# Second expert layer of a fused attention and two-layer MLP kernel: slices over two chunks, six accumulators, single units

## The chip, the cores and the metric

One core of one Trainium2 chip runs the whole program in one launch. The metric is device time in microseconds. The engines have a queue each and run it in order: TensorE (PE in the rows, its weight loads PEld), VectorE (DVE), ScalarE (ACT), GpSimd (POOL) and SyncE (SP), whose queue here issues DMAs.

## What is computed

```python
attn = attention(q, k, v)              # q is averaged over pairs of rows first
x = attn as (1152 tokens, 512)
h = x @ w_in;  g = P(h) / Q(h);        x = g @ w_out      # first expert layer, d_ff 2048
h = x @ w2_in; g = max(h,0) + log1p(exp(-|h|)); out = g @ w2_out   # second expert layer
```

The weights come as 64-bit floats and are made into 32-bit pairs on the chip (below: decoding). Every product is made from a high and a low part of both factors, in three matmuls: high by high, low by high, high by low.

## The kernel before

After attention (to about 340 us) both expert layers run over three chunks `c` of 384 tokens (`NCH`, `TOK`) and 16 slices `f` of 128 hidden columns (`NF`), of which the first eight (`FH`) make the first half. A *unit* is one (c, f). For a unit, `up` (L600) makes h with 12 matmuls of 384 columns (4 blocks of the model dimension by three products); the activation follows on ScalarE and VectorE; `down1` (L648, 12 matmuls of 384 columns) or `down2` (L692, 9 of 512 columns) adds the unit to accumulators in PSUM. Units are taken in pairs of neighbouring slices of one chunk: h is a tile of two PSUM banks (L602) with two buffers, and an activation works on 768 columns at once.

In the first layer an activation is long. ScalarE runs `act1_a` (L625 to L628), VectorE `act1_y` (L633, L635, L634; the last frees h), ScalarE Ln and Exp (L639, L640), VectorE the products L644, L645, L646, then ScalarE makes the high part gh (L620) and VectorE the low part gl (L621, shown as L122, the line of the helper `sub`). Downs follow their ups by two pairs. At a chunk's end `end1` (L672) adds up the halves (L678), and ScalarE and VectorE split the sum into xh and xl for the next layer. In the second layer the activation is one softplus (L689), gh (L620) and gl (L122), and downs follow by one pair.

The second layer's first half today takes its units chunk by chunk: chunk 2 with slices 0 to 7, then chunk 1, then chunk 0 (L832). The accumulators of one chunk are three banks of four; at the end of a chunk's first half `half2` (L704) copies them to SBUF.

Decoding a weight tile is: a load of 512 KB into one of two raw buffers (L162 for w_in, L167 for w_out); a scaled copy on ScalarE (L174 in and after the last pair of the first layer, L176 before); L182, L185 (only after L174) and L188 on VectorE; then the split: a cast on ScalarE (L198) and a subtraction (L199, shown as L122). `w_step` (L758) does one piece of each for successive tiles: split one, convert the next, copy the one after, load the one after that. Three things call it: `w_pace` in the first layer, by the rates r0 (first half) and r1 (second half), in steps per hundred units; the rate r2 in the second layer; and `w_need`, which repeats it until a tile that is used next has been split. The subtraction of a split runs on VectorE in the first layer and on GpSimd from the last pair of the first layer on (L760).

The order of instructions on each engine is set by a scheduler, which moves them against the order in which the code issues them; `tc.high_priority` and `behind` (L112: issue after a named instruction) steer it. Each engine then runs its list in that order.

Of the kernel before, what the change touches and what calls it, by code (L numbers as in the profile page):

```python
# [7 lines left out]
F32 = mybir.dt.float32  # L8
# [61 lines left out]
    pra=0,  # L70
    k1=1,
    r0=50,
    r1=60,
    r2=60,
    whd=0,
    dup=2,
    qsp=0,
# [9 lines left out]
def attn_moe_kernel(tc, q, k, v, w1_in, w1_out, moe_a, moe_b, w2_in, w2_out, out):  # L87
# [24 lines left out]
    def behind(fn, *engines):  # L112
        with ExitStack() as es:
            for e in engines:
                es.enter_context(tc.issue_after(st["last", e]))
            fn()

    def sb(**kw):
        return tc.alloc_tile_pool(reuse_waits="tile", **kw)

    def sub(eng, o, a, b):
        return eng.tensor_tensor(out=o, in0=a, in1=b, op=ALU.subtract)  # L122
# [69 lines left out]
    def w_split(i, pool, lo):  # L192
        g = st.pop(("pk", i)).bitcast(F32)
        w = pool.tile([128, 2, 512], F32R, tag="w", name="w")
        if T["whd"] and i % T["whd"] == 0:
            nc.vector.tensor_copy(out=w[:, 0], in_=g)
        else:
            nc.scalar.copy(out=w[:, 0], in_=g)  # L198
        sub(lo, w[:, 1], g, w[:, 0])  # L199
        st["w", order[i]] = w  # L200
        st["wp", order[i]] = pool
# [392 lines left out]
    def xcols(c):  # L594
        return slice(c * TOK, (c + 1) * TOK)

    def T_(nm, bufs, dt=F32):
        return ap.tile([128, 2, TOK], dt, tag=nm, name=nm, bufs=bufs)

    def up(m, c, f):  # L600
        if f % 2 == 0:
            st["h"] = ph_.tile([128, 2, 512], F32, tag="h", name="h")[:, :, 0:TOK]  # L602
        h = st["h"][:, f % 2]
        w = st["w", (m, 0, f)]
        n = 0
        for d in range(ND):
            wd = slice(d * 128, (d + 1) * 128)
            for wi, x in ((0, xh), (1, xh), (0, xl)):
                nc.tensor.matmul(out=h, lhsT=w[:, wi, wd], rhs=x[:, d, xcols(c)],  # L609
                                 start=(n == 0), stop=(n == 3 * ND - 1))  # L610
                n += 1
        return st["h"]
# [1 line left out]
    def pick(key, n):  # L614
        return T[key][n % len(T[key])]

    def split(p, es=(slice(0, 2),)):
        gh, gl = T_("gh", 2, F32R), T_("gl", 2, F32R)
        for e in es:
            nc.scalar.copy(out=gh[:, e], in_=p[:, e])  # L620
            sub(nc.vector, gl[:, e], p[:, e], gh[:, e])  # L621
        return gh, gl

    def act1_a(h):
# [58 lines left out]
                    nc.scalar.copy(out=xh[:, d, xcols(c)], in_=t)  # L683
                sub(nc.vector, xl[:, d, xcols(c)], t, xh[:, d, xcols(c)])

    def act2(h, es=(slice(0, 2),)):
        p = T_("p", 2)
        for e in es:
            nc.scalar.activation(out=p[:, e], in_=h[:, e], func=AF.Softplus)  # L689
        return split(p, es)  # L690

    def down2(c, f, gh, gl, ts=(0, 1, 2)):  # L692
        first = f == 0 or (f == FH and c > 0)
        last = f == NF - 1 or (f == FH - 1 and c > 0)
        if first:
            for t in range(TOK // 128):
                st["acc", c, t] = pa_.tile([128, DM], F32, tag="acc", name="acc")
        w = st["w", (1, 1, f)]
        for t in ts:
            for n, (g, wi) in enumerate(((gh, 0), (gh, 1), (gl, 0))):  # L700
                nc.tensor.matmul(out=st["acc", c, t], lhsT=g[:, t * 128:(t + 1) * 128], rhs=w[:, wi],  # L701
                                 start=(first and n == 0), stop=(last and n == 2))

    def half2(c):  # L704
        p = st["part2", c] = pt2[c - 1].tile([128, TOK // 128, DM], F32, name=f"part2{c}")
        for t in range(TOK // 128):
            acc = st.pop(("acc", c, t))
            with tc.high_priority():
                if t == 1:
                    nc.vector.tensor_copy(out=p[:, t], in_=acc)  # L710
                else:
                    nc.scalar.copy(out=p[:, t], in_=acc)
# [16 lines left out]
    if True:  # L729
# [27 lines left out]

        def w_step():  # L758
            if cnt["split"] < cnt["conv"] and freed:
                w_split(cnt["split"], freed.pop(0), nc.gpsimd if "second" in st else nc.vector)  # L760
                cnt["split"] += 1
            if cnt["conv"] < cnt["abs"]:
                for n in range(3):
                    w_conv(cnt["conv"], n)
                cnt["conv"] += 1
            if cnt["abs"] < cnt["load"] and cnt["abs"] - cnt["split"] < 2:
                w_abs(cnt["abs"])
                cnt["abs"] += 1
            if cnt["load"] < len(order) and cnt["load"] - cnt["conv"] < 2:
                w_load(cnt["load"])  # L770
                cnt["load"] += 1

        def w_need(t):
            while cnt["split"] <= order.index(t):
                w_step()
# [11 lines left out]
        def every(n, rate):  # L787
            return (n + 1) * rate // 100 > n * rate // 100
# [40 lines left out]
                g1.pop(k - LAG1)  # L829
        pt_.release()  # L830
        pt2 = [sb(name=f"part2{c}", bufs=1) for c in range(2)]
        units = [(c, f) for c in reversed(range(NCH)) for f in range(FH)]  # L832
        units += [(c, f) for c in range(NCH) for f in range(FH, NF)]
        g2 = {}
        for k in range(NG + LAG2):
            if k < NG:
                for e, (c, f) in enumerate(units[2 * k:2 * k + 2]):
                    if c == (NCH - 1 if f < FH else 0):
                        w_need((1, 0, f))
                    h = up(1, c, f)  # L840
                    if f < FH and c == 0:
                        freed.append(st["wp", (1, 0, f)])
                    if e == 0 and every(2 * k, T["r2"]):
                        w_step()
                g2[k] = act2(h, (slice(0, 2),) if k < NG - 1 else (slice(0, 1), slice(1, 2)))
                if every(2 * k + 1, T["r2"]):
                    w_step()
            if k >= LAG2:
                for e, (c, f) in enumerate(units[2 * (k - LAG2):2 * (k - LAG2) + 2]):
                    if c == (NCH - 1 if f < FH else 0):  # L850
                        w_need((1, 1, f))
                    if c < NCH - 1 or f < NF - LAST:
                        gh, gl = g2[k - LAG2]
                        down2(c, f, gh[:, e], gl[:, e])
                        if f < FH and c == 0:
                            freed.append(st["wp", (1, 1, f)])
                        if f == FH - 1 and c:
                            half2(c)
                        if f == NF - 1:
                            for t in range(TOK // 128):  # L860
                                end2(c, t)
        for t in range(TOK // 128):
            for n in range(NU - LAST, NU):
                gh, gl = g2[n // 2]
                down2(*units[n], gh[:, n % 2], gl[:, n % 2], ts=(t,))
            end2(NCH - 1, t)
        pt2[1].release()
        pt2[0].release()
# [39 lines left out]
```

## Time and profile before

| | us |
|---|---|
| runs, median of three | 758.01 (754.85 to 762.01) |
| profiled execution | 755.56 |
| its span, first to last instruction | 753.8 |
| TensorE busy in the span | 726.2 (96%) |
| VectorE, ScalarE, GpSimd busy | 545.4, 494.4, 262.2 |

The span is 753.8 us of the profiled execution's 755.56; 1.8 us lie around it. Busy time is the union of an engine's instructions. Attention ends at about 340 us, the first expert layer at 551 us, and the second fills the rest. In a timeline, rows of the same kind that follow each other are merged (x2, x8), a bracket gives the engine's idle time just before the row and what ended it, and "q" rows are an engine's sequencer.

### The profile page before, as it was taken

Reading aid. Unit: us, or ns where it says so; the run is one execution under the profiler, and the core shown is the slowest. Engines: PE = TensorE matmul, PEld = TensorE weight load, DVE = VectorE, ACT = ScalarE, POOL = GpSimd, SP = SyncE. Lnnn points to the kernel's source line nnn. Section 1 sums busy time; section 2 is a strip of 40 time slices with the busy share of each in tenths; the row PEclk is TensorE's granted clock in tenths of the full one; section 3 lists DMA queues with packets and bytes.
Section 4 is the critical chain, followed back from the end, with each engine's and each line's share of the span. In section 5 each row is a group of like instructions: output and inputs, shape, how many; then the busy total and the mean of one; then the engine's idle time right before and its main releaser. Section 6 shows DMA issues by size and latency. Waiting matters only on the chain.

```text
span 753.8 us, 11735 instructions
## 1 busy us (share of the span) xinstructions
PE 726.2 (96%) x4273; PEld 682.4 (91%) x4273; DVE 545.4 (72%) x906; ACT 494.4 (66%) x921; POOL 262.2 (35%) x212
## 2 busy tenths in 40 slices
PE   8999999999999998887999999999999899999998
PEld 5699999999999998777999999999889779989996
DVE  6877778787867679988999999999987772111122
ACT  3278888888888889988767777876744452222121
POOL 5278796969697875000000000000233431000000
PEclk9999999999999999998999999999999999999999
DMA  4876383737353434331202122221224440001011
GB/s 131 205 154 153 94 188 84 185 85 185 84 126 85 98 99 127 125 128 57 84 29 80 61 84 62 81 82 56 85 93 138 138 137 0 1 1 43 0 43 43
DMA packets 60474, 70.32 MB, mean 93 GB/s; under 512 B 20008, under 2 KB 48512, under 8 KB 60416
## 3 DMA queue, kind: packets, MB, share of 16 engines
q1 hardware_dynamic: 59232, 68.58, 34.0%
q10 hardware_dynamic: 1184, 0.98, 0.4%
q8 instruction: 34, 0.56, 0.3%
q14 instruction: 24, 0.20, 0.1%
HBM read 47.71 MB, written 2.36 MB: 66 GB/s over the span
## 4 chain that ended last, share of the span: by engine, by line
PE 78%; DVE 11%; ACT 6%; issue 2%; DMA 2%; POOL 0%; DVEq 0%; ACTq 0%; SPq 0%
PE h L609 20%; PE p L396 11%; PE acc L659 11%; PE acc L701 10%; PE s L446 5%; PE s L447 5%; PE pv L471 5%; PE pv L469 4%; PE pv L470 4%; DVE pk L188 2%; DMA wraw<-in_moe_w_in_dram 2%; ACT p L450 1%; ACT ph L457 1%; DVE pk L182 1%; DVE pk L185 1%
## 5 line engine op out<-in xcount | busy, mean ns | idle before, releaser
L609 PE MATMUL h<-xh,w 128*128 128x384 f32 x768 | 198.9, 338 | 7.4 <-DVE p L634 7.4
L122 POOL TENSOR_TENSOR pl<-p,ph 128x576 fp32r<-128x576 f32 x126 | 181.4, 1453 | 55.0 <-ACT ph L457 35.5
L609 PEld LDWEIGHTS h<-xh,w 128*128 128x128 f32 x768 | 140.6, 190 | 10.2 <-issue 8.3
L401 DVE TENSOR_REDUCE nm<-p 128x1 f32<-128x384 f32 x216 | 117.0, 552 | 44.9 <-PE p L396 43.4
L450 ACT ACTIVATE p<-s 128x288 f32<-128x288 f32 x288 | 114.9, 408 | 28.4 <-PE s L447 26.6
L609 PE MATMUL h<-xl,w 128*128 128x384 f32 x384 | 129.8, 338 | 0.0
L122 POOL TENSOR_TENSOR w<-pk,w 128x512 fp32r<-128x512 f32 x23 | 35.6, 1549 | 252.2 <-PE h L609 187.4
L122 DVE TENSOR_TENSOR gl<-p,gh 128x768 fp32r<-128x768 f32 (+1 forms) x49 | 48.2, 988 | 98.1 <-ACT gh L620 98.0
L457 ACT CAST ph<-p 128x576 fp32r<-128x576 f32 x144 | 96.8, 672 | 2.5
L701 PE MATMUL acc<-w,gh 128*128 128x512 f32 x288 | 90.3, 395 | 2.4 <-ACT gh L620 1.7
L659 PE MATMUL acc<-gh,w 128*128 128x384 f32 x384 | 91.2, 336 | 0.0
L471 PE MATMUL pv<-pl,v 128*128 128x288 f32 x288 | 87.2, 303 | 1.7 <-DVE pl L122 1.3
L469 PE MATMUL pv<-ph,v 128*128 128x288 f32 x288 | 87.2, 303 | 1.2 <-ACT ph L457 1.0
L470 PE MATMUL pv<-ph,v 128*64 128x288 f32 x288 | 85.7, 298 | 0.0
L689 ACT ACTIVATE p<-h 128x768 f32<-128x768 f32 (+1 forms) x25 | 19.5, 783 | 90.0 <-PE h L609 90.0
L609 PEld LDWEIGHTS h<-xl,w 128*128 128x128 f32 x384 | 72.9, 190 | 0.0
L659 PEld LDWEIGHTS acc<-gh,w 128*128 128x128 f32 x384 | 68.7, 188 | 0.3 <-ACT gh L620 0.2
L701 PEld LDWEIGHTS acc<-w,gh 128*128 128x128 f32 x288 | 53.5, 188 | 14.1 <-ACT gh L620 2.5
L471 PEld LDWEIGHTS pv<-pl,v 128*128 128x128 f32 x288 | 55.0, 191 | 5.0 <-DVE pl L122 3.9
L659 PE MATMUL acc<-gl,w 128*128 128x384 f32 x192 | 58.1, 337 | 0.8 <-DVE gl L122 0.8
L701 PE MATMUL acc<-w,gl 128*128 128x512 f32 x144 | 57.1, 396 | 1.3 <-DVE gl L122 1.3
L469 PEld LDWEIGHTS pv<-ph,v 128*128 128x128 f32 x288 | 55.6, 193 | 2.5 <-ACT ph L457 2.4
(148 smaller groups left out, 1478.6 us busy)
## 6 DMA issues: line engine op xcount, KB each, us to landing
wraw<-in_moe_w_in_dram SPq DMA_DIRECT2D x32, 512.0 KB
wraw<-in_moe_w_out_dram SPq DMA_DIRECT2D x32, 512.0 KB
vr<-in_v_dram SPq DMA_DIRECT2D x8, 576.0 KB
kr<-in_k_dram SPq DMA_DIRECT2D x15, 288.0 KB
qr<-in_q_dram SPq DMA_DIRECT2D x15, 256.0 KB
out_dram<-m SPq DMA_DIRECT2D x15, 128.0 KB
kha<-ks0a SPq DMA_DIRECT2D x4, 288.0 KB
khb<-ks0b SPq DMA_DIRECT2D x4, 288.0 KB
```

The source lines that it names most:

```text
L122: return eng.tensor_tensor(out=o, in0=a, in1=b, op=ALU.subtract)
L396: m = nc.tensor.matmul(out=o, lhsT=l, rhs=r, start=(a == 0), stop=(a == len(mm) - 1))
L401: nc.vector.tensor_reduce(out=st["nm", j][:, t, e:e + 1], in_=st.pop(("p1", j, u)), axis=AX.X, op=ALU.max, negate=True)
L446: nc.tensor.matmul(out=t, lhsT=KS[i][x][:, ks], rhs=QQ[i][x][:, cs], start=True, stop=False)
L450: st["last", "exp"] = nc.scalar.activation(out=st["p"][:, s % 2], in_=t, func=AF.Exp).ins
L457: nc.scalar.copy(out=ph, in_=p)
L469: nc.tensor.matmul(out=st["pv", j, g], lhsT=h, rhs=ph, start=(c == 0), stop=False)
L470: nc.tensor.matmul(out=st["pv", j, g][0:64], lhsT=l, rhs=ph, start=False, stop=False)
L471: nc.tensor.matmul(out=st["pv", j, g], lhsT=h, rhs=pl, start=False, stop=(c == C - 1))
L609: nc.tensor.matmul(out=h, lhsT=w[:, wi, wd], rhs=x[:, d, xcols(c)], start=(n == 0), stop=(n == 3 * ND - 1))
L659: nc.tensor.matmul(out=st["acc", c, d], lhsT=w[:, wi, wd], rhs=g, start=(first and n == 0), stop=(last and n == 2))
L701: nc.tensor.matmul(out=st["acc", c, t], lhsT=g[:, t * 128:(t + 1) * 128], rhs=w[:, wi], start=(first and n == 0), stop=(last and n == 2))
```

## The change

- The second layer gets its own up (`up2`, one PSUM bank per unit) and activation (`act2`, 384 columns per unit); p, gh and gl stay tiles for a pair, of which each unit takes a half. Downs follow two units behind.
- The PSUM pools are released after the first layer and made anew: two banks for h, six for accumulators, so two chunks can be open.
- First half: slice by slice over chunks 2 and 1, then chunk 0 with all eight slices. The second half's order stays.
- One `w_step` at most per unit, issued behind gh (`behind`), r2 90 (was 60), r1 40 (was 60). `w_need` stays.
- The subtraction of every split runs on VectorE.

```diff
-    r1=60,
-    r2=60,
+    r1=40,
+    r2=90,
...
+    def up2(c, f):
+        h = ph_.tile([128, 512], F32, tag="h2", name="h2")[:, 0:TOK]
+        w = st["w", (1, 0, f)]
+        mm = [(wi, x, d) for d in range(ND) for wi, x in ((0, xh), (1, xh), (0, xl))]
+        for n, (wi, x, d) in enumerate(mm):
+            nc.tensor.matmul(out=h, lhsT=w[:, wi, d * 128:(d + 1) * 128], rhs=x[:, d, xcols(c)],
+                             start=(n == 0), stop=(n == len(mm) - 1))
+        return h
+
+    def act2(n, h):
+        if n % 2 == 0:
+            st["g2"] = T_("p", 2), T_("gh", 2, F32R), T_("gl", 2, F32R)
+        p, gh, gl = (t[:, n % 2] for t in st["g2"])
+        nc.scalar.activation(out=p, in_=h, func=AF.Softplus)
+        st["last", "gh"] = nc.scalar.copy(out=gh, in_=p).ins
+        sub(nc.vector, gl, p, gh)
+        return gh, gl
...
-                w_split(cnt["split"], freed.pop(0), nc.gpsimd if "second" in st else nc.vector)
+                w_split(cnt["split"], freed.pop(0), nc.vector)
...
+        pa_.release()
+        ph_.release()
+        ph_ = sb(name="ph2", bufs=2, space=PSUM)
+        pa_ = sb(name="pa2", bufs=2 * (TOK // 128), space=PSUM)
-        units = [(c, f) for c in reversed(range(NCH)) for f in range(FH)]
+        units = [(c, f) for f in range(FH) for c in (2, 1)]
+        units += [(0, f) for f in range(FH)]
...
+        for n in range(NU + 2 * LAG2):
+            if n < NU:
+                c, f = units[n]
+                if c == (NCH - 1 if f < FH else 0):
+                    w_need((1, 0, f))
+                g2[n] = act2(n, up2(c, f))
+                if f < FH and c == 0:
+                    freed.append(st["wp", (1, 0, f)])
+                if every(n, T["r2"]):
+                    behind(w_step, "gh")
+            m = n - 2 * LAG2
+            if m >= 0:
+                c, f = units[m]
+                if c == (NCH - 1 if f < FH else 0):
+                    w_need((1, 1, f))
+                if c < NCH - 1 or f < NF - LAST:
+                    down2(c, f, *g2[m])
```

Lines of the program after the change differ by a few: L609 stays for the first layer's up, L690 is the second layer's; L658 and L712 are the downs; L698 and L699 softplus and gh; L643 to L645 the products.

How it moves instructions, first on TensorE at the end of the first layer. The last pair of that layer has h_6777 before and h_6741 after; the downs of w_5780 belong to the pair two before it, and h_6957 is the second layer's first pair. Before:

```order
L609 MATMUL h_6777<-xh_69,w_5696 128x384 x2
L609 MATMUL h_6777<-xl_70,w_5696 128x384
L609 MATMUL h_6957<-xh_69,w_6173 128x384 x2
L609 MATMUL h_6957<-xl_70,w_6173 128x384
L609 MATMUL h_6957<-xh_69,w_6173 128x384 x2
L609 MATMUL h_6957<-xl_70,w_6173 128x384
L609 MATMUL h_6957<-xh_69,w_6173 128x384 x2
L609 MATMUL h_6957<-xl_70,w_6173 128x384
L609 MATMUL h_6957<-xh_69,w_6173 128x384 x2
L609 MATMUL h_6957<-xl_70,w_6173 128x384
L609 MATMUL h_6957<-xh_69,w_6249 128x384 x2
L659 MATMUL acc_6749<-gh_6743,w_5780 128x384 x2
```

After:

```order
L609 MATMUL h_6741<-xh_69,w_5696 128x384 x2
L609 MATMUL h_6741<-xl_70,w_5696 128x384
L609 MATMUL h_6741<-xh_69,w_5696 128x384 x2
L609 MATMUL h_6741<-xl_70,w_5696 128x384
L658 MATMUL acc_6713<-gh_6707,w_5780 128x384 x2
L658 MATMUL acc_6714<-gh_6707,w_5780 128x384 x2
L658 MATMUL acc_6715<-gh_6707,w_5780 128x384 x2
L658 MATMUL acc_6716<-gh_6707,w_5780 128x384 x2
L658 MATMUL acc_6713<-gl_6708,w_5780 128x384
L658 MATMUL acc_6714<-gl_6708,w_5780 128x384
```

Where 14 ups of the second layer stood between the last up of the first and the next downs, the downs follow at once. From the first finished accumulator of chunk 1 to the first matmul of the layer's last down pair (w_6081 before, w_6088 after) TensorE's list has 166 matmuls before and 146 after; on the way stand, before, 166 = 9 + 22 + 10 + 24 + 14 + 14 + 24 + 5 + 8 + 5 + 2 + 16 + 13, and after, 146 = 9 + 24 + 8 + 6 + 16 + 18 + 24 + 8 + 6 + 16 + 11 (runs of one tile or one pair).

ScalarE in the second layer's first half, around one softplus (L689) before:

```order
L198 CAST w<-pk 128x512 x2
L174 ACTIVATE pk<-wraw 128x512
L689 ACTIVATE p<-h 128x768
L620 CAST gh<-p 128x768
L174 ACTIVATE pk<-wraw 128x512
L198 CAST w<-pk 128x512 x2
L174 ACTIVATE pk<-wraw 128x512
L198 CAST w<-pk 128x512
L689 ACTIVATE p<-h 128x768
```

and two units of it after (L698):

```order
L698 ACTIVATE p<-h_7033 128x384
L699 CAST gh<-p 128x384
L198 CAST w<-pk 128x512
L174 ACTIVATE pk<-wraw 128x512
L698 ACTIVATE p<-h_7071 128x384
L699 CAST gh<-p 128x384
L198 CAST w<-pk 128x512
L174 ACTIVATE pk<-wraw 128x512
```

Casts and copies of the decoding stood before and after the softplus in changing number; now one cast and one copy follow each gh.

VectorE in the same half, from one gl to the next but one before:

```order
L122 TENSOR_TENSOR gl<-p,gh 128x768
L182 TENSOR_SCALAR pk<-pk 128x512
L185 SCALAR_TENSOR_TENSOR pk<-wraw,pk 128x512
L188 SCALAR_TENSOR_TENSOR pk<-wraw,pk 128x512
L182 TENSOR_SCALAR pk<-pk 128x512
L185 SCALAR_TENSOR_TENSOR pk<-wraw,pk 128x512
L188 SCALAR_TENSOR_TENSOR pk<-wraw,pk 128x512
L182 TENSOR_SCALAR pk<-pk 128x512
L185 SCALAR_TENSOR_TENSOR pk<-wraw,pk 128x512
L122 TENSOR_TENSOR gl<-p,gh 128x768
```

and after:

```order
L122 TENSOR_TENSOR gl<-p,gh 128x384
L122 TENSOR_TENSOR w<-pk,w 128x512
L182 TENSOR_SCALAR pk<-pk 128x512
L185 SCALAR_TENSOR_TENSOR pk<-wraw,pk 128x512
L188 SCALAR_TENSOR_TENSOR pk<-wraw,pk 128x512
L122 TENSOR_TENSOR gl<-p,gh 128x384
L122 TENSOR_TENSOR w<-pk,w 128x512
L182 TENSOR_SCALAR pk<-pk 128x512
L185 SCALAR_TENSOR_TENSOR pk<-wraw,pk 128x512
L188 SCALAR_TENSOR_TENSOR pk<-wraw,pk 128x512
```

Eight of decoding's instructions stood between two gl of a pair each (with the subtraction on GpSimd); now four stand between two gl of a unit each, the subtraction among them. After the last xl of the first layer VectorE's list has 25 such splits, one behind the gl of each unit from the second on, with two units left out.

## Rows read from the trace of the kernel before

**Rows 1.** busy us by stage: PE, PEld, DVE, ACT, POOL (instructions), clock, DMA share

```profile
500.00:620.00 120.00, 112.79 (x589) 103.36 (x588) 104.22 (x135) 69.59 (x104) 31.23 (x20) 1.00 0.33 106
```

**Rows 2.** TensorE's timeline at layer 1's end: start, length, instructions, idle before, releaser

```profile
519.06 0.34 PE L609 MATMUL h<-xl,w 128*128 128x384 f32 x1
...
520.90 0.59 PE L609 MATMUL h<-xh,w 128*128 128x384 f32 x2 [1.49 <-DVE p L634]
...
546.39 1.61 PE L659 MATMUL acc<-gh,w 128*128 128x384 f32 x8
```

**Rows 3.** chain of waits: start, length; one group of downs, one of ups

```profile
625.11 4.19 PE acc L701 x18
629.30 4.17 PE h L609 x24
```

**Rows 4.** waits in 480:640: who waited for whom, us in total, times, longest

```profile
PE h L609 <- DVE p L634: 2.7, 2, 1.5
...
PE acc L659 <- DVE gl L122: 0.8, 2, 0.6
```

**Rows 5.** TensorE's timeline: first row of four down groups, layer 2

```profile
586.40 0.62 PE L701 MATMUL acc<-w,gh 128*128 128x512 f32 x2
...
596.75 0.74 PE L701 MATMUL acc<-w,gh 128*128 128x512 f32 x2 [0.69 <-ACT gh L620]
...
607.37 0.73 PE L701 MATMUL acc<-w,gh 128*128 128x512 f32 x2 [1.00 <-ACT gh L620]
...
616.67 0.63 PE L701 MATMUL acc<-w,gh 128*128 128x512 f32 x2
```

**Rows 6.** ScalarE's timeline around one late softplus, layer 2

```profile
593.56 0.62 ACT L198 CAST w<-pk 128x512 fp32r<-128x512 f32 x1 [2.41 <-DVE pk L188]
594.46 0.67 ACT L174 ACTIVATE pk<-wraw 128x512 f32<-128x512 f32 x1 [0.28 <-DMA wraw<-in_moe_w_out_dram]
595.03 0.79 ACT L689 ACTIVATE p<-h 128x768 f32<-128x768 f32 x1
595.86 0.83 ACT L620 CAST gh<-p 128x768 fp32r<-128x768 f32 x1
```

**Rows 7.** VectorE's timeline from chunk 1's adds on, layer 1's end

```profile
514.04 2.12 DVE L678 TENSOR_TENSOR part<-acc,part 128x384 f32<-128x384 f32 x4 [0.62 <-PE acc L659]
...
517.95 0.95 DVE L633 TENSOR_TENSOR p<-h,p 128x768 f32<-128x768 f32 x1
...
518.82 1.01 DVE L635 SCALAR_TENSOR_TENSOR m<-s,b_sb,m 128x768 f32<-128x768 f32 x1
...
521.53 0.69 DVE L122 TENSOR_TENSOR w<-pk,w 128x512 fp32r<-128x512 f32 x1
...
522.81 0.95 DVE L122 TENSOR_TENSOR gl<-p,gh 128x768 fp32r<-128x768 f32 x1
...
523.68 1.28 DVE L188 SCALAR_TENSOR_TENSOR pk<-wraw,pk 128x512 int32<-128x512 int32 x2
...
524.88 1.01 DVE L644 SCALAR_TENSOR_TENSOR p<-p,a_sb,s 128x768 f32<-128x768 f32 x1
...
526.68 0.95 DVE L633 TENSOR_TENSOR p<-h,p 128x768 f32<-128x768 f32 x1
```

**Rows 8.** VectorE twice, then GpSimd, from their timelines

```profile
527.55 2.02 DVE L635 SCALAR_TENSOR_TENSOR m<-s,b_sb,m 128x768 f32<-128x768 f32 x1
...
588.68 1.18 DVE L188 SCALAR_TENSOR_TENSOR pk<-wraw,pk 128x512 int32<-128x512 int32 x1
...
527.45 1.31 POOL L122 TENSOR_TENSOR w<-pk,w 128x512 fp32r<-128x512 f32 x1 [187.45 <-PE h L609]
```

**Rows 9.** groups by form in 735:754, halved tiles: count, busy us, mean ns, idle before

```profile
L122 DVE TENSOR_TENSOR gl<-p,gh 128x384 fp32r<-128x384 f32 x2 | 1.0, 553 | 6.9 <-ACT gh L620 6.9
...
L620 ACT CAST gh<-p 128x384 fp32r<-128x384 f32 x2 | 0.9, 520 | 0.0
...
L689 ACT ACTIVATE p<-h 128x384 f32<-128x384 f32 x2 | 0.9, 489 | 6.6 <-PE h L609 6.6
```

More of the change, by code (lines that the diff above doesn't have):

```diff
@@ L615, in pick, with split @@
         return T[key][n % len(T[key])]
-    def split(p, es=(slice(0, 2),)):
+    def split(p):
         gh, gl = T_("gh", 2, F32R), T_("gl", 2, F32R)
-        for e in es:
-            nc.scalar.copy(out=gh[:, e], in_=p[:, e])
-            sub(nc.vector, gl[:, e], p[:, e], gh[:, e])
+        nc.scalar.copy(out=gh, in_=p)
+        sub(nc.vector, gl, p, gh)
         return gh, gl
@@ L684, in end1 @@
                 sub(nc.vector, xl[:, d, xcols(c)], t, xh[:, d, xcols(c)])
[L686 to L690, printed above, removed]
+    def up2(c, f):
[12 more added lines that the diff above has]
+        st["last", "gh"] = nc.scalar.copy(out=gh, in_=p).ins
+        sub(nc.vector, gl, p, gh)
+        return gh, gl
     def down2(c, f, gh, gl, ts=(0, 1, 2)):
@@ L831, in attn_moe_kernel @@
         pt2 = [sb(name=f"part2{c}", bufs=1) for c in range(2)]
-        units = [(c, f) for c in reversed(range(NCH)) for f in range(FH)]
+        pa_.release()
[4 more added lines that the diff above has]
+        units += [(0, f) for f in range(FH)]
         units += [(c, f) for c in range(NCH) for f in range(FH, NF)]
         g2 = {}
[L835 to L840, printed above, removed]
-                    if f < FH and c == 0:
[L842 to L861, printed above, removed]
@@ new lines, in attn_moe_kernel @@
+        for n in range(NU + 2 * LAG2):
[15 more added lines that the diff above has]
+                    down2(c, f, *g2[m])
+                    if f < FH and c == 0:
+                        freed.append(st["wp", (1, 1, f)])
+                    if f == FH - 1 and c:
+                        half2(c)
+                    if f == NF - 1:
+                        for t in range(TOK // 128):
+                            end2(c, t)
@@ L862, in attn_moe_kernel @@
         for t in range(TOK // 128):
             for n in range(NU - LAST, NU):
-                gh, gl = g2[n // 2]
-                down2(*units[n], gh[:, n % 2], gl[:, n % 2], ts=(t,))
+                down2(*units[n], *g2[n], ts=(t,))
             end2(NCH - 1, t)
```

## The prediction

> **What bounds the kernel now.** I read the whole-span page first: TensorE is busy 96% of the span, and TensorE leads the chain that ended last. So only time in which TensorE stands still can be won, and I looked for that by stages. After 500 us the edit's stretch shows it: from 500 to 620 TensorE is busy 112.79 of 120 us at a granted clock of 1.00 [rows 1]. After 620 its groups follow each other without a stop, as in [rows 3], up to the drain at the very end, which the edit leaves as it is.
>
> Idle time understates a stall. Up and down matmuls start one every 0.174 us (24 in 4.17 us) and 0.233 us (18 in 4.19 us) at full rate [rows 3], but each shows 0.34 to 0.4 us of duration, so part of every stop is hidden under the tail of the matmul before it. At 519.06 one matmul starts, the next at 520.90: 1.84 us less 0.17 is 1.67 us lost, where 1.49 us of idle is shown [rows 2]. I therefore count starts.
>
> The Trainium skill says the same in "Perfetto Trace Analysis", section "Identifying the Most-Contended Engine": busy time of matmuls is a poor measure, since pipelined matmuls look smaller. By busy time alone 7.2 us could be won in 500:620, by starts 9.4.
>
> There are two places.
> - *The end of the first expert layer*, four stops: two that wait 2.7 us for VectorE's L634, which frees the h buffer, and two that wait 0.8 us (0.2 and 0.6) for VectorE's split gl [rows 4]. With 0.18 us more for each, 4.2 us. VectorE is the late one there.
> - *The first half of the second layer.* A pair of units at full rate takes 4.17 + 4.19 = 8.36 us [rows 3]. The starts of the down groups from 586.40 on lie 10.35, 10.62 and 9.30 us apart [rows 5], so 1.99 + 2.26 + 0.94 = 5.2 us are lost. The ScalarE rows say how: the softplus of a pair starts at 595.03, directly behind a decode step. The cast at 593.56 had stood 2.41 us for VectorE's L188, the L174 at 594.46 waited for its load, and softplus and gh came after them in the queue [rows 6]. The matmuls that wait name gh and gl; the weights themselves are there.
>
> **The change part by part.**
>
> *Order of slices and of decoding.* Today eight units of chunk 2 need 16 weights in 8 x 4.18 = 33 us, in bursts from `w_need`, and the order printed above lets one to three decode steps stand ahead of a softplus or a gl. Afterwards a slice serves two chunks, so 16 weights are wanted in 16 units, and each unit has one fixed group: softplus, gh, then cast and L174 on ScalarE; gl, then split, L182, L185, L188 on VectorE. Cost per unit, from the halved tiles [rows 9] and the decode rows: ScalarE 0.49 + 0.52 + 0.62 + 0.67 = 2.3 us, VectorE 0.55 + 0.60 + 0.34 + 0.64 + 0.64 = 2.8 us [rows 6, 7], both under the unit's 4.18 us of TensorE. What hides their length: h(n) must be free only when the up of unit n+2 starts, which is 9 + 12 + 9 matmuls or 6.3 us after h(n) is full; less softplus, 5.8 us of slack. gh and gl have 2.1 us more. I take all 5.2 us as won.
>
> What two halved operations cost over a whole one is inside the 2.3 and 2.8 us, and is nothing as long as the 5.8 us stand.
>
> *The load in the loop.* Two raw buffers remain. A load starts when L188 of the weight two before is done: L188 at 588.68 ends at 589.86, and the L174 that waited for the load behind it starts at 594.46, 4.6 us [rows 6, 8]. In the new order the weight's L182 stands behind its L174 of the same unit, so the ring is 4.6 + 0.67 + 0.34 + 0.64 + 0.64 = 6.9 us in two units, 8.36 us. It does not close; 1.4 us are to spare.
>
> *The end of the first layer.* Here the edit gives and takes. It takes cover: h of layer 2 is one unit now and not a pair, with two buffers either way, so two units of look-ahead stand where four stood. Counted in the order, between the first finished accumulator of chunk 1 and the first matmul of the layer's last down pair lie 166 matmuls before and 146 after (the PE rows above show 14 ups of h_6957 that no longer stand ahead of a down). The count reproduces the trace: 166 x 0.174 = 28.9 us, plus the three stops in it, 2.7 + 0.2 + 3 x 0.18 = 3.4 us, is 32.3; the trace has 514.04 to 546.39, 32.35 us [rows 2, 7]. After: 146 x 0.174 = 25.4 us.
>
> What it gives: VectorE has less to decode (r1 falls from 60 to 40) and GpSimd does no split. VectorE's work in that stretch, in the new order, by start-to-start times [rows 7]: adds and xl of chunk 1 3.91; for each of three pairs y and the last product 3.58, L643 and L644 1.80, gl 0.87, which is 6.25, together 18.75 (the last gl drops out, that of the pair before comes in); one split and two L182 1.28; two L185 and two L188 at 0.60, 2.40; then ScalarE's gh, 0.83 [rows 6], and some 0.1 of hand-over, an estimate. Sum 27.3 us against 25.4: the last pair's downs come 1.9 us late in all, and its gl some 0.2 more. So about 2.1 us of stops stay where 4.2 were; 2.1 us won.
>
> The lengths above are undisturbed ones. L635 took 2.02 us at 527.55, while GpSimd ran its split from 527.45, and 1.01 us at 518.82 with GpSimd idle [rows 7, 8]. With GpSimd's splits gone I take the short one; with a lengthening of that size left in two of the three pairs, the 2.1 us won shrink to nothing.
>
> The Trainium skill ("SBUF — State Buffer", section "Who interferes with whom") names one shared port pair, which VectorE and GpSimd take from each other for a whole instruction. The pair of rows agrees with it, and by it the short lengths hold.
>
> *PSUM.* Six accumulators and two single h fill what four accumulators and two double h filled. Layer 2's first down needs banks that end1's adds of chunk 0 still read; 19 ups (3.3 us) stand between, the adds take 2.1 us [rows 7]. half2 gets two units (8.4 us with downs) before its banks are wanted. Nothing lost; without that cover about 2 us once.
>
> *Sum:* 5.2 + 2.1 = 7.3 us. The profiled execution took 755.56 us, so 748.3 in its terms. It lies 2.45 us under the median of the runs shown, 758.01; by that median **750.7 us**.
>
> **The rivals.**
> - *The shorter look-ahead eats the gain.* If VectorE's stretch is as long as before (32.35 us against 25.4 of matmuls), the stops there are 7 us and not 2.1: net 5.2 - 2.8 = 2.4 us, 755.6. For it: VectorE is the releaser of all four stops today. Against: its doubled rows fall on GpSimd's splits, and the new order has fewer decode rows there. Half of it gives 753.
> - *Stops only move.* The softplus is no longer late, but as much is lost elsewhere, say in `w_need` at the second half's start or where chunks change: 757 to 760. Against: the order shows each weight's split several units ahead of its use.
> - *Slower: the load ring closes.* Place: L174 on ScalarE, behind which the next softplus queues, and L182 on VectorE, behind which the next gl queues. If softplus, gh, cast and split were in the ring too it would be 6.9 + 0.49 + 0.52 + 0.62 + 0.60 = 9.1 us, 4.56 per unit; over 25 units 9.5 us are lost, less the 5.8 us of slack 3.7, so 754.4. It ends 1% slower when some 15 us are lost net: 25 units of 5.0 us, a ring of 10.0, loads of 5.5 us. That gives 765.6. For it: two loads may share the DMA engines. Against: the order puts L182 in its own unit, and 4.6 us was the longest of the rows I use.
>
> **How the numbers follow.** Forecast 0.60, shorter look-ahead 0.20, stops only move 0.13, ring 0.07. The forecast's own range is 748 to 753. The runs shown reach from 754.85 to 762.01, so even a median scatters by some 2 us; with that and the second case 746 to 757.5 leaves out less than 2 in 10. One per cent, about what a measurement here can tell from no change, is a time under 750.4; the forecast lies on that edge, a little under half of it (0.28) beyond, and 0.04 of the look-ahead case: faster 0.32. Slower 0.06, from the ring and the scatter of the third case. Within 1% 0.62.
>
> **What would show it.** Right: starts of down groups 4.18 us apart from the first unit of layer 2 on, no ScalarE wait for VectorE's L188 ahead of a softplus, GpSimd idle after 340 us, and some 2 us of stops left at the last two or three down pairs of layer 1, waiting for gh. Wrong: L174 waiting for its load unit after unit with softplus late behind it; over 4 us of stops at the layer's end; or VectorE operations still doubled with GpSimd idle.

## The result

The changed kernel takes 749.24 us, median of four runs (747.76 to 750.27), beside 757.56 us of the kernel before (four runs): a ratio of 0.9896, interval 0.9876 to 0.9917. Run again later it came to 0.9885 (0.9872 to 0.9897). It is a little over 1% faster. The profiled run took 748.41 us, with a span of 746.6 us where 753.8 stood.

Where the time went is read as ahead of the prediction, from starts. From the first matmul of the first layer's first up to the start of TensorE's last row, the trace of before takes 419.2 us and that of after 412.1 us: 7.1 us less, all of it between 500 and 620 us. The busy time by stage, for after, answers to [rows 1]:

```profile
500.00:620.00 120.00, 118.72 (x626) 110.41 (x625) 96.50 (x151) 69.81 (x117) 0.00 (x0) 1.00 0.28 88
```

TensorE is busy 118.72 us of the 120 where it was 112.79. GpSimd, the fifth engine of the row, has nothing left to do there (31.23 us before).

TensorE's timeline at the end of the first layer holds all that still stands, answering to [rows 2, 4]:

```profile
527.19 0.34 PE L609 MATMUL h<-xl,w 128*128 128x384 f32 x1
528.31 1.67 PE L658 MATMUL acc<-gh,w 128*128 128x384 f32 x8 [0.78 <-ACT gh L619]
...
533.15 1.68 PE L658 MATMUL acc<-gh,w 128*128 128x384 f32 x8 [0.23 <-ACT gh L619]
...
536.15 0.98 PE L658 MATMUL acc<-gl,w 128*128 128x384 f32 x4 [0.28 <-DVE gl L122]
```

Three stops. From start to start and less the 0.174 us of a matmul (the first: 528.31 less 527.19 less 0.17) they cost 0.95 + 0.39 + 0.45 = 1.79 us, where four cost 4.26 us before. Two wait for ScalarE's gh, one for gl; no up waits for VectorE any more.

In the second layer no matmul waits for anything. The first rows of four neighbouring down groups, TensorE's timeline, answer to [rows 5]:

```profile
577.90 0.62 PE L712 MATMUL acc<-w,gh 128*128 128x512 f32 x2
...
582.08 0.62 PE L712 MATMUL acc<-w,gh 128*128 128x512 f32 x2
...
586.26 0.62 PE L712 MATMUL acc<-w,gh 128*128 128x512 f32 x2
...
590.44 0.63 PE L712 MATMUL acc<-w,gh 128*128 128x512 f32 x2
```

They lie 4.18 us apart, unit by unit, which is half of the 8.36 us that a pair takes at full rate. One unit on ScalarE, from its timeline, answers to [rows 6]:

```profile
573.92 0.49 ACT L698 ACTIVATE p<-h 128x384 f32<-128x384 f32 x1 [2.05 <-PE h L690]
574.45 0.51 ACT L699 CAST gh<-p 128x384 fp32r<-128x384 f32 x1
574.86 0.62 ACT L198 CAST w<-pk 128x512 fp32r<-128x512 f32 x1
575.38 0.68 ACT L174 ACTIVATE pk<-wraw 128x512 f32<-128x512 f32 x1
```

and on VectorE, from its own:

```profile
574.99 0.56 DVE L122 TENSOR_TENSOR gl<-p,gh 128x384 fp32r<-128x384 f32 x1 [1.18 <-ACT gh L699]
575.51 0.69 DVE L122 TENSOR_TENSOR w<-pk,w 128x512 fp32r<-128x512 f32 x1
576.12 0.42 DVE L182 TENSOR_SCALAR pk<-pk 128x512 int32<-128x512 int32 x1
576.58 0.69 DVE L185 SCALAR_TENSOR_TENSOR pk<-wraw,pk 128x512 int32<-128x512 int32 x1
577.30 0.69 DVE L188 SCALAR_TENSOR_TENSOR pk<-wraw,pk 128x512 int32<-128x512 int32 x1
```

The softplus waits 2.05 us for its own up and for nothing else, gh follows at once, and the decode step stands behind both. ScalarE spends 2.3 us on the unit and VectorE 3.0 us, by the rows; both have time over.

### The profile page after: what moved, and what is told of

Read it like the earlier page. It is cut to its first block, busy times and chain, and to the rows that moved or that the text cites. A ratio compares the mean times of both kernels' runs of the same rounds, so it can differ in the third digit from the quotient of the medians.

```text
span 746.6 us, 11768 instructions
## 1 busy us (share of the span) xinstructions
PE 725.7 (97%) x4273; PEld 683.5 (92%) x4273; DVE 551.6 (74%) x956; ACT 502.0 (67%) x967; POOL 227.2 (30%) x189
## 4 chain that ended last, share of the span: by engine, by line
PE 86%; DVE 7%; ACT 5%; issue 1%; POOL 0%; DVEq 0%; ACTq 0%
PE acc L712 13%; PE h L690 13%; PE p L396 11%; PE acc L658 11%; PE h L609 11%; PE s L446 5%; PE s L447 5%; PE pv L471 4%; PE pv L469 4%; PE pv L470 4%; ACT p L450 1%; ACT ph L457 1%; PE wm L264 1%; PE tk L327 1%; DVE w L122 1%
## 5 line engine op out<-in xcount | busy, mean ns | idle before, releaser
L122 DVE TENSOR_TENSOR gl<-p,gh 128x384 fp32r<-128x384 f32 (+1 forms) x72 | 49.6, 689 | 93.3 <-ACT gh L699 92.3
L609 PE MATMUL h<-xh,w 128*128 128x384 f32 x384 | 100.8, 341 | 4.2 <-DVE p L633 4.2
L690 PE MATMUL h<-xh,w 128*128 128x384 f32 x384 | 97.8, 336 | 0.0
L698 ACT ACTIVATE p<-h 128x384 f32<-128x384 f32 x48 | 23.6, 492 | 109.5 <-PE h L690 109.4
L658 PE MATMUL acc<-gh,w 128*128 128x384 f32 x384 | 93.0, 337 | 1.0 <-ACT gh L619 1.0
L712 PE MATMUL acc<-w,gh 128*128 128x512 f32 x288 | 90.0, 394 | 0.0
L609 PEld LDWEIGHTS h<-xh,w 128*128 128x128 f32 x384 | 71.1, 192 | 4.5 <-issue 4.5
L690 PEld LDWEIGHTS h<-xh,w 128*128 128x128 f32 x384 | 70.2, 188 | 3.9
L658 PEld LDWEIGHTS acc<-gh,w 128*128 128x128 f32 x384 | 68.7, 188 | 2.1 <-ACT gh L619 2.0
L609 PE MATMUL h<-xl,w 128*128 128x384 f32 x192 | 65.3, 340 | 0.0
L690 PE MATMUL h<-xl,w 128*128 128x384 f32 x192 | 64.6, 337 | 0.0
L712 PEld LDWEIGHTS acc<-w,gh 128*128 128x128 f32 x288 | 53.5, 188 | 9.0
L658 PE MATMUL acc<-gl,w 128*128 128x384 f32 x192 | 59.7, 338 | 0.3 <-DVE gl L122 0.3
```

Of the source, the lines that this page charges most:

```text
L658: nc.tensor.matmul(out=st["acc", c, d], lhsT=w[:, wi, wd], rhs=g, start=(first and n == 0), stop=(last and n == 2))
L690: nc.tensor.matmul(out=h, lhsT=w[:, wi, d * 128:(d + 1) * 128], rhs=x[:, d, xcols(c)], start=(n == 0), stop=(n == len(mm) - 1))
```

## The experiments

All columns but the ratio come from the profiled execution of each kernel. A stop is a row of TensorE's timeline with idle time ahead of it, counted from start to start as above; "first to last" runs from the first up of layer 1 to TensorE's last row. That up starts between 330.2 and 332.5 us in these profiles, behind attention, which no edit touches; the column leaves that scatter out.

| kernel | ratio to before (95%) | stops, end of layer 1 | stops, layer 2 | first to last |
|---|---|---|---|---|
| before | 1 | 4.26 | 4.82 | 419.2 |
| changed | 0.9896 (0.9876 to 0.9917) | 1.79 | 0 | 412.1 |
| e1 changed, chunk by chunk | 0.9913 (0.9886 to 0.9940) | 1.79 | 0 | 412.6 |
| e2 changed, steps not fixed | 0.9903 (0.9875 to 0.9932) | 1.79 | 0 | 412.3 |
| e3 before, decoding as in the changed | 0.9869 (0.9845 to 0.9894) | 0 | 0 | 409.7 |
| e4 changed, r1 60 | 0.9947 (0.9920 to 0.9973) | 5.50 | 0 | 416.2 |
| e5 before, splits on VectorE | 0.9906 (0.9881 to 0.9930) | 2.00 | 0 | 412.0 |
| e6 before, steps fixed | 0.9926 (0.9903 to 0.9949) | 4.29 | 0 | 413.0 |
| e7 changed, splits on GpSimd | 0.9945 (0.9929 to 0.9962) | 2.71 | 0 | 413.7 |
| e8 changed, r1 20 | 0.9924 (0.9905 to 0.9942) | 2.54 | 0 | 413.8 |
| e9 before, r1 40 | 1.0010 (0.9997 to 1.0023) | 2.30 | 6.81 | 421.3 |
| e10 e3 with r2 60 | 0.9889 (0.9873 to 0.9906) | 0 | 0.36 | 410.3 |
| e11 changed, two ups early | 0.9887 (0.9872 to 0.9903) | 1.36 | 0 | 411.4 |
| e12 changed again | 0.9885 (0.9872 to 0.9897) | 1.78 | 0 | 412.3 |

### Is it the order of slices? (e1)

```diff
-        units = [(c, f) for f in range(FH) for c in (2, 1)]
+        units = [(c, f) for c in (2, 1) for f in range(FH)]
```

> The changed kernel with one line of its list of units set back: the second layer's first half takes chunk 2 with slices 0 to 7, then chunk 1, then chunk 0. Units, banks, fixed decode steps and rates stay. Theory A (the slice order wins layer 2's 5.2 us, since 16 weights in 8 units of chunk 2 force bursts of decoding): the bursts come back, starts of the down groups lie over 4.18 us apart in chunk 2, about 5 us are lost, 754.4 us. Theory B (one fixed decode step behind each gh wins them, and the weights decoded ahead are enough for either order): ScalarE's and VectorE's lists show one step per unit here too, so TensorE goes on without a stop, 749.2 us.

749.93 us, no stop in layer 2, and the same three stops before it. Theory A falls: chunk 2 finds its weights without bursts. Layer 2 begins with 39 weights split, and one step per unit keeps ahead of either order.

### Is it the fixed place of the steps? (e2)

```diff
-                    behind(w_step, "gh")
+                    w_step()
```

> The changed kernel with the decode steps issued where the code calls them and not behind gh, so that the scheduler places them; all else stays. Theory B (the fixed place of the steps is the cause): VectorE's list has up to 7 decode instructions between two gl where 4 stood, softplus and gl come late again; at the end of layer 1 VectorE's stretch has 3 splits, 3 L182, 3 L185, 3 L188 (6.5 us) where 1, 2, 2, 2 stood (3.7 us), with one gl less (0.9 us), so some 2 us more are lost there, and 1 to 4 us in layer 2: 752 to 755 us. Theory C (units of 384 columns and six accumulators are the cause, wherever the steps stand): 749 us.

749.47 us, the same stops. In this kernel the fixed place isn't needed either, and theory B's loss at the end of layer 1 didn't come, though VectorE's list there has three splits where one stood: the rows that came in stand behind the last product L645, and up to it there are seven decode rows in either kernel. So neither of the two parts, undone alone, gives the 5 us back. Either the units and banks win it, or the splits on VectorE do, or several parts each suffice.

### The decoding alone, on the kernel before (e3)

```diff
-            nc.scalar.copy(out=gh[:, e], in_=p[:, e])
+            st["last", "gh"] = nc.scalar.copy(out=gh[:, e], in_=p[:, e]).ins
...
-                    if e == 0 and every(2 * k, T["r2"]):
-                        w_step()
...
-                if every(2 * k + 1, T["r2"]):
-                    w_step()
+                for n in (2 * k, 2 * k + 1):
+                    if every(n, T["r2"]):
+                        behind(w_step, "gh")
...
-                w_split(cnt["split"], freed.pop(0), nc.gpsimd if "second" in st else nc.vector)
+                w_split(cnt["split"], freed.pop(0), nc.vector)
```

and r1 40, r2 90.

> The kernel before with pairs of units, double banks and the order chunk by chunk kept, and only the decoding changed: both steps of a pair issued behind its gh, r1 40, r2 90, splits on VectorE. Theory B (decoding is the cause): layer 2's 5.2 us are won here too, and the boundary keeps its 166 matmuls, 28.9 us, against VectorE's 3.9 + 18.75 + 5.2 us of decoding + 0.9 = 28.8 us, so all 4.2 us of its stops but about 0.2 go: 747 us, under the changed kernel. Theories A and C (slice order, units, banks): layer 2 keeps its stops of 5.2 us, and the boundary alone is won, 753 us.

746.35 us, and TensorE waits nowhere after 500 us. Pairs, double banks and the old order lose nothing once the decoding is changed: slices, units and six accumulators won none of the 7.1 us. They even cost the 1.79 us that stay. VectorE's timeline shows it. Rows of e3 (chunk 1's adds, then the product L646 of two pairs):

```profile
513.20 2.12 DVE L678 TENSOR_TENSOR part<-acc,part 128x384 f32<-128x384 f32 x4
...
526.15 0.96 DVE L646 SCALAR_TENSOR_TENSOR p<-m,p 128x768 f32<-128x768 f32 x1
...
538.73 0.95 DVE L646 SCALAR_TENSOR_TENSOR p<-m,p 128x768 f32<-128x768 f32 x1
```

and the same three of the changed kernel, where L646 is L645:

```profile
513.49 2.12 DVE L677 TENSOR_TENSOR part<-acc,part 128x384 f32<-128x384 f32 x4
...
526.45 0.94 DVE L645 SCALAR_TENSOR_TENSOR p<-m,p 128x768 f32<-128x768 f32 x1
...
539.01 0.95 DVE L645 SCALAR_TENSOR_TENSOR p<-m,p 128x768 f32<-128x768 f32 x1
```

Every row of the changed kernel stands 0.28 to 0.30 us behind that of e3. VectorE works at the same pace; only TensorE has other work meanwhile. Its timeline in e3, the three rows that answer to the three stops:

```profile
528.47 1.57 PE L659 MATMUL acc<-gh,w 128*128 128x384 f32 x8
...
533.17 1.57 PE L659 MATMUL acc<-gh,w 128*128 128x384 f32 x8
...
536.32 0.88 PE L659 MATMUL acc<-gl,w 128*128 128x384 f32 x4
```

No bracket, so no wait. In TensorE's list of e3, 42 ups of the second layer stand ahead of layer 1's last down pair (8 of them ahead of the first of these rows), in that of the changed kernel 17 (none ahead of its first stop). The 8 alone are 1.4 us, more than the 0.95 us of that stop.

### The two halves of the decoding, each alone (e5, e6)

e5 is the kernel before with one line:

```diff
-                w_split(cnt["split"], freed.pop(0), nc.gpsimd if "second" in st else nc.vector)
+                w_split(cnt["split"], freed.pop(0), nc.vector)
```

e6 is the kernel before with the first three pieces of e3's diff, of which the core is

```diff
-                    if e == 0 and every(2 * k, T["r2"]):
-                        w_step()
...
-                if every(2 * k + 1, T["r2"]):
-                    w_step()
+                for n in (2 * k, 2 * k + 1):
+                    if every(n, T["r2"]):
+                        behind(w_step, "gh")
```

> The kernel before with one edit: all splits on VectorE, none on GpSimd; rates, places of the steps, pairs and order stay. Theory F (GpSimd's splits slow VectorE's decoding, so the cast waits for L188 and softplus behind it): layer 2's 5.2 us are won; at layer 1's end VectorE has 5 splits, 6 L182, 2 L185, 5 L188 (9.3 us) where 8.0 us and some 1 us of lengthening stood, so its stops stay at some 4.5 us: 752.5 us beside 757. Theory B (the unfixed place of the steps): VectorE's list has 7 to 10 decode instructions between two gl where 6 to 9 stood, layer 2 keeps its stops: 757 us or more.

> The kernel before with one edit: the steps of the second layer are issued behind the gh of their pair; r1 60, r2 60, GpSimd's splits, pairs and order stay. Theory B (the place of the steps): VectorE's list has three decode instructions between most gl where 6 to 9 stood, and ScalarE's has softplus, gh, cast, copy; layer 2's 5.2 us are won, the end of layer 1, whose lists are the same up to there, keeps its 4.2 us: 752 us. Theory F (GpSimd): the stops in layer 2 stay for the most part, 755 to 757 us.

748.13 and 749.47 us. Each alone clears layer 2. e6 leaves the end of layer 1 as it was, as it should, since its lists there are the same (4.29 us, the same four waits for L634 and gl). e5 halves them, 4.26 to 2.00 us, which I had put at no change. So theories B and F both hold: layer 2's stops need GpSimd's splits *and* steps that may stand ahead of a softplus. How GpSimd's splits bring them about is shown less fully, since the scheduler ordered ScalarE's and VectorE's lists anew in e5: how much of its gain is shorter rows and how much the new order was not separated. What GpSimd does to VectorE is to be seen in the kernel before, just ahead of the late softplus of [rows 6]. GpSimd's timeline:

```profile
591.23 1.75 POOL L122 TENSOR_TENSOR w<-pk,w 128x512 fp32r<-128x512 f32 x1 [1.92 <-ACT w L198]
```

and VectorE's:

```profile
591.86 1.67 DVE L188 SCALAR_TENSOR_TENSOR pk<-wraw,pk 128x512 int32<-128x512 int32 x1
```

L188 runs while GpSimd splits and takes 1.67 us; the cast that waited 2.41 us for it starts at 593.56, and the softplus is queued behind that cast. By groups over 553 to 620, before (columns: count, busy us, mean ns, idle before):

```profile
L122 POOL TENSOR_TENSOR w<-pk,w 128x512 fp32r<-128x512 f32 x16 | 24.2, 1512 | 44.5 <-ACT w L198 42.0 <-issue 2.5
...
L188 DVE SCALAR_TENSOR_TENSOR pk<-wraw,pk 128x512 int32<-128x512 int32 x18 | 18.9, 1052 | 0.5
...
L185 DVE SCALAR_TENSOR_TENSOR pk<-wraw,pk 128x512 int32<-128x512 int32 x18 | 13.4, 746 | 0.6
...
L182 DVE TENSOR_SCALAR pk<-pk 128x512 int32<-128x512 int32 x18 | 11.8, 655 | 14.0 <-ACT pk L174 14.0
```

and e5, splits on VectorE:

```profile
L122 DVE TENSOR_TENSOR w<-pk,w 128x512 fp32r<-128x512 f32 x20 | 13.7, 687 | 4.3 <-ACT w L198 4.2
L185 DVE SCALAR_TENSOR_TENSOR pk<-wraw,pk 128x512 int32<-128x512 int32 x19 | 13.1, 690 | 0.5
L188 DVE SCALAR_TENSOR_TENSOR pk<-wraw,pk 128x512 int32<-128x512 int32 x19 | 13.1, 690 | 0.4
...
L182 DVE TENSOR_SCALAR pk<-pk 128x512 int32<-128x512 int32 x18 | 7.6, 425 | 8.2 <-ACT pk L174 8.1
```

Per weight VectorE's three decode rows take on average 0.66 + 0.75 + 1.05 = 2.45 us where GpSimd does the splits; without it they take 0.43 + 0.69 + 0.69 = 1.80, and the split on VectorE 0.69, together 2.49. The split on GpSimd saved VectorE next to nothing. And L188 comes earlier, which the wait of the cast shows, from the table of waits over the same stretch (total us, times, longest), before:

```profile
ACT w L198 <- DVE pk L188: 20.5, 10, 2.9
```

and in e5:

```profile
ACT w L198 <- DVE pk L188: 12.2, 11, 2.1
```

The loads are not what changed: L174's waits for them, by the same tables, come to 12.7 us in 10 waits before and 13.5 us in 11 waits in e5, which has no stop in layer 2.

L635 had shown the two engines side by side already [rows 8]. The Trainium skill's "SBUF — State Buffer", section "Who interferes with whom", has one shared port pair for the two as the only contention; the groups above agree, since with GpSimd idle every decode row returns to its short length.

### GpSimd in the changed kernel (e7)

```diff
-                w_split(cnt["split"], freed.pop(0), nc.vector)
+                w_split(cnt["split"], freed.pop(0), nc.gpsimd if "second" in st else nc.vector)
```

> The changed kernel with the subtraction of the splits on GpSimd again from the last pair of layer 1 on. Theory F (GpSimd's splits lengthen VectorE's instructions beside them): VectorE's stretch at the end of layer 1 loses one split (0.6 us) and one gl (0.9 us) and wins two lengthenings of 1 us, so the stops stay at 1.8 to 2.5 us; in layer 2 VectorE has 2.2 us of work per unit and up to 1.3 us of lengthening, under 4.18 us, no stop: 749 to 750 us. If GpSimd's splits are the cause by themselves, wherever the steps stand: stops of 5 us in layer 2, 754 us.

751.80 us. Layer 2 stays free of stops, as expected; at the end of layer 1 there are four stops now, 2.71 us by start to start, the two largest:

```profile
531.06 1.68 PE L658 MATMUL acc<-gh,w 128*128 128x384 f32 x8 [1.06 <-ACT gh L619]
...
538.86 0.98 PE L658 MATMUL acc<-gl,w 128*128 128x384 f32 x4 [0.50 <-DVE gl L122]
```

A little more than expected; with the smaller stretches between them first to last grows by 1.6 us. That isn't the price of GpSimd alone: the scheduler also put fewer matmuls on TensorE between chunk 1's first add and layer 1's last down pair, 137 where the changed kernel's trace has 144, which is 1.2 us.

### The rate r1 (e4, e8, e9)

Each changes one number: e4 and e8 in the changed kernel, e9 in the kernel before.

```diff
-    r1=40,
+    r1=60,
```

```diff
-    r1=40,
+    r1=20,
```

```diff
-    r1=60,
+    r1=40,
```

> The changed kernel with r1 at 60 again. Theory D (VectorE's list sets the stops at the end of layer 1): from chunk 1's adds to chunk 0's VectorE has 6 splits, 6 L182, 3 L185, 5 L188 (10.5 us) where 1, 2, 2, 2 stood (3.7 us), and one product more (0.9 us); its stretch grows from 27.3 to 35.0 us against 25.4 us of matmuls, so stops of 9.6 us where 1.8 are: 757 us. Rival (the steps hide beside ScalarE's waits and cost little): 749 to 751 us.

> The changed kernel with r1 at 20, so that no decode instruction stands in VectorE's list between chunk 1's adds and chunk 0's (3.7 us before); 35 weights instead of 39 are split by then, and w_need issues a few steps more in layer 2, one or two per unit. Theory D (VectorE's list against 25.4 us of matmuls): its stretch falls from 27.3 to 23.6 us, the 1.8 us of stops go, 747.4 us. Rival (ScalarE's chain of Ln, Exp and gh sets the stops): they stay, 749 us; or the missing weights stop layer 2: over 750 us.

> The kernel before with one number changed: r1 at 40 instead of 60; GpSimd's splits and the unfixed steps stay. VectorE's list between chunk 1's adds and chunk 0's has 4 L182, 5 L185, 4 L188 (6.8 us) where 2 splits, 6 L182, 3 L185, 5 L188 stood (8.0 us), and one product less (0.9 us), so about 2 us of the 4.3 us of stops at the end of layer 1 go, if r1 is what the boundary's gain comes from; layer 2 keeps its 5 us, since GpSimd's splits and the unfixed steps are both there: 754 to 755 us. If GpSimd's splits are the larger part of the boundary's stops, less than 1 us is won: 756 us.

e4: 751.84 us. TensorE's stops:

```profile
521.24 0.59 PE L609 MATMUL h<-xh,w 128*128 128x384 f32 x2 [1.49 <-DVE p L633]
...
532.58 1.67 PE L658 MATMUL acc<-gh,w 128*128 128x384 f32 x8 [2.75 <-ACT gh L619]
...
537.90 1.68 PE L658 MATMUL acc<-gh,w 128*128 128x384 f32 x8 [0.74 <-ACT gh L619]
```

5.50 us where theory D expected 9.6. The direction holds, the size doesn't: about 3.3 us of the decode rows that I added up stand in VectorE's list behind the last product L645, where they delay nothing, and from chunk 1's first add to layer 1's last down pair TensorE has 153 matmuls where the changed kernel's trace has 144, 1.6 us more to do meanwhile.

e8: 750.43 us, not 747.4. VectorE's stretch has no decode row left, yet the stops are 2.54 us, the longest 1.73 us where the changed kernel has 0.95 us. TensorE's timeline:

```profile
529.78 1.32 PE L658 MATMUL acc<-gh,w 128*128 128x384 f32 x6 [1.56 <-ACT gh L619]
```

Without decode rows the scheduler wrote ScalarE's list differently. ScalarE's timeline:

```profile
520.74 0.94 ACT L638 ACTIVATE s<-m,onep 128x768 f32<-128x768 f32 x1 [3.27 <-DVE m L634]
521.63 0.99 ACT L625 ACTIVATE p<-h,a_sb 128x768 f32<-128x768 f32 x1
522.52 0.84 ACT L639 ACTIVATE s<-s 128x768 f32<-128x768 f32 x1
```

and VectorE's:

```profile
523.39 1.02 DVE L643 SCALAR_TENSOR_TENSOR p<-p,a_sb,s 128x768 f32<-128x768 f32 x1 [1.88 <-ACT s L639]
```

L625 of the next pair stands between Ln (L638) and Exp (L639), Exp is 0.9 us later, and VectorE idles 1.88 us for it. A pair's way from h to gh crosses between the two engines four times. From the first add to the last product VectorE idles 3.0 us for ScalarE, where it idled nowhere in the changed kernel, so its stretch, from chunk 1's first add (VectorE)

```profile
514.98 1.94 DVE L677 TENSOR_TENSOR part<-acc,part 128x384 f32<-128x384 f32 x4
```

to the end of the last pair's gh (ScalarE),

```profile
540.31 0.83 ACT L619 CAST gh<-p 128x768 fp32r<-128x768 f32 x1 [3.00 <-DVE p L645]
```

takes 26.2 us, not 23.6; in the changed kernel it takes 27.4. And TensorE's list changed too: from that add to layer 1's last down pair it has 133 matmuls where the changed kernel's trace has 144, 1.9 us less. Counted from that add, the last gh comes 1.2 us sooner and TensorE has 1.9 us less to do before it, so the stops grow, by 0.75 us. Theory D as a sum over one engine against a fixed count of matmuls falls: it left out ScalarE's sequence, and the scheduler changed the count. How a list without decode rows and with the old sequence would do wasn't tried.

e9: 757.74 us, no gain. The end of layer 1 wins what was expected (4.26 to 2.30 us), but four weights fewer are split by then, 37 where 41 were, and layer 2, with GpSimd and unfixed steps, stops for longer, twice within 2 us here:

```profile
615.27 0.73 PE L701 MATMUL acc<-w,gh 128*128 128x512 f32 x2 [1.18 <-ACT gh L620]
617.10 0.50 PE L701 MATMUL acc<-w,gl 128*128 128x512 f32 x1 [1.10 <-DVE gl L122]
```

Six stops are 6.81 us in all. Two of them, 1.41 and 1.28 us, wait for neither gh nor gl but for `half2`'s copy on VectorE (L710), which is queued behind an L185 of 1.66 us and an L188 of 1.79 us, each begun while GpSimd was splitting. What r1 spares VectorE in one layer comes back in the next, unless the next is mended too.

### The rate r2 (e10)

e3 with one number set back:

```diff
-    r2=90,
+    r2=60,
```

> The kernel before with the steps behind gh, r1 40 and splits on VectorE, as in the run before_pinned, but r2 left at 60. Theory (r2 does not matter, since w_need makes up for missing steps and TensorE has slack): no stop after 500 us, as with r2 90, 746 to 747 us. Rival (w_need's steps are not held behind gh; one place of VectorE's list has 11 decode instructions between two gl, 6.3 us of a pair's 8.4): a stop of 1 to 3 us in layer 2, 748 us.

746.26 us in the profiled run, a ratio of 0.9889, and one stop in layer 2, for a weight whose cast is late:

```profile
558.27 1.57 PE L701 MATMUL acc<-w,gh 128*128 128x512 f32 x4 [0.19 <-ACT w L198]
```

0.36 us, and first to last 0.6 us over that of e3. r2 is worth that much or nothing. The intervals of e3's ratio (0.9869) and of this one overlap.

### Cover ahead of the last downs (e11, e12)

```diff
-                g2[n] = act2(n, up2(c, f))
+                with tc.high_priority() if n < 2 else ExitStack():
+                    h = up2(c, f)
+                g2[n] = act2(n, h)
```

> The changed kernel with one edit: the first two ups of the second layer are issued under high priority, which puts 24 of its matmuls, where 6 stood, between the downs of layer 1's last pairs; VectorE's list stays, but for two decode steps more. Theory (cover ahead of the last downs is what is short, 17 ups of layer 2 where the pinned kernel before has 42): the second and third stop (0.4 and 0.45 us) and what follows them go, the first (0.95 us), ahead of which the lists are the same, stays: 748.2 us. Rival (VectorE is late by as much whatever stands on TensorE): the same stop, moved behind the ups, 749.2 us.

> The changed kernel itself, as a yardstick on the same chip for the three runs beside it: 749.2 us, 0.990 of the kernel before.

748.28 us for e11 and 747.91 us for e12. Cover is work that TensorE can do before the downs that wait. First to last falls by 0.8 us from e12 to e11; as ratios, 0.9885 and 0.9887, the two can't be told apart. TensorE's stops in e11:

```profile
530.22 1.68 PE L658 MATMUL acc<-gh,w 128*128 128x384 f32 x8 [0.78 <-ACT gh L619]
...
535.06 1.66 PE L658 MATMUL acc<-gh,w 128*128 128x384 f32 x8 [0.24 <-ACT gh L619]
```

The third stop is gone, the first stays. The second stays too, against what I wrote: 24 ups were moved, but behind the 32 downs in which it lies, so it has no cover. The stop that got cover went and the ones that got none stayed, by as much as they were.

## Why the prediction was right

**The sum.** 5.2 + 2.1 = 7.3 us were forecast; the traces show 7.1. In profiled terms 748.3 us against 748.41. The median, 749.24, lies 1.5 us under the 750.7 forecast, since I added the 2.45 us by which the profiled execution of before lay under the median of its runs; for the changed kernel that gap is 0.83 us. "Within 1%" had the larger chance; the measured 0.9896 is just outside it, on the edge where the text had put the forecast, and its interval reaches inside. That stops are counted by starts rests on the rows here, each 0.34 us long at one every 0.174 us; the reason that the page of the Trainium skill cited there gives ("Perfetto Trace Analysis", section "Identifying the Most-Contended Engine"), that pipelined matmuls look smaller, is a different one, and no run here shows it.

**Layer 2's first half, 5.2 us: right in size, wrong in cause.** The step "Order of slices and of decoding" gave the gain to the new order, under which 16 weights are wanted in 16 units and not in 8. e1 takes the order back and loses nothing. Of that step only the second half holds, the fixed group behind each gh, and even that isn't needed once GpSimd is out (e2). What won the 5.2 us is either of two edits of the decoding (e5, e6). I had the row with the cast waiting 2.41 us for L188, and the row with an operation doubled beside GpSimd [rows 6, 8], and didn't put them together: I used the doubling for layer 1's end alone. The size was read off the stops, so any cause that clears them all would have given it; that the number came out owes as much to luck as to the mechanism.

Nor did all five stops wait for gh or gl, as the prediction says. Inside the first interval of [rows 5], 10.35 us, stands one of 0.93 us for `half2`'s copies of chunk 2's accumulators. TensorE's timeline of before:

```profile
588.02 0.73 PE L701 MATMUL acc<-w,gh 128*128 128x512 f32 x2 [0.71 <-ACT part L712]
```

and ScalarE's:

```profile
586.30 0.67 ACT L174 ACTIVATE pk<-wraw 128x512 f32<-128x512 f32 x1 [1.34 <-DMA wraw<-in_moe_w_in_dram]
...
587.38 1.07 ACT L712 COPY part<-acc 128x512 f32<-128x512 f32 x2
```

The copies stood in the queue behind a decode step that waited for its load. This stop, too, is gone in e5 and in e6.

**The end of layer 1, 2.1 us won, 2.1 left: right (2.5 and 1.8).** VectorE's stretch was put at 27.3 us; from chunk 1's adds at 513.49 to the end of the last pair's gh it takes 27.4. The parts come apart by the experiments: splits on VectorE alone bring 4.26 to 2.00 (e5), r1 40 alone brings it to 2.30 (e9), the whole decoding to 0 (e3), and the smaller look-ahead puts 1.79 back. The first rival, "the shorter look-ahead eats the gain", thus named a real mechanism, but its price is 1.8 us in all, and the sum had counted it. But the sum is only good where the lists of all three engines stay as they are: it gave 9.6 us for e4 (5.50 measured) and 0 for e8 (2.54), where ScalarE's sequence and TensorE's count of matmuls had changed.

**PSUM.** That two single banks cut the look-ahead is only half of it: they would allow 24 ups ahead, and the scheduler placed 17. e11 has 24 and is 0.8 us shorter by its trace.

**The load ring: right.** L174 waits for its load twice in layer 2's first half, 1.3 and 0.4 us, and no softplus is late for it. "Stops only move" didn't happen.

**A better kernel.** e3, the kernel before with the decoding alone changed, has no stop after 500 us and is 2.4 us shorter than the changed kernel from first to last. Its ratio of 0.9869 lies under the changed kernel's 0.9896 and 0.9885, but the intervals overlap: by the trace it is shorter than both, by its time it is faster than the kernel before and not told apart from the changed one.

## What to carry to other kernels

Undo a change's parts one by one even when the sum comes out: here the parts that name it won nothing and cost 1.8 us, and two small ones, either of which was enough, won layer 2. Before work is put on GpSimd to unburden VectorE, add what VectorE's instructions lengthen by beside it. And where a stop is short of cover, look at which matmuls stand ahead of the very downs that wait; work placed after them doesn't help.

## What was not expected of the hardware

A split of 128x512 took 1.51 us on GpSimd and 0.69 on VectorE, and the lengthening beside it cost VectorE 0.65 us per weight, about as much as doing the split itself. The lengthening falls on the cheapest instruction too: L182 took 0.43 us with GpSimd idle, 0.66 on average in the kernel before, and 1.06 at 572.17, begun while GpSimd was splitting. GpSimd's own rows stretch as well: the same split took 1.29 us at its shortest in the kernel before and 3.11 at 544.05.
